# A causal convolution moved to token-major output, with one transposing transfer per block in place of a bounce through DRAM

## The chip, the cores and the metric

One core of one Trainium2 chip. The metric is the device time of one execution in microseconds; medians of several executions are quoted.

Engines in the profile: PE is TensorE (matmul), PEld its weight load, DVE VectorE, ACT ScalarE, POOL GpSimd, SP SyncE (here it only issues transfers). PEclk is the granted clock of TensorE as a share of full speed.

## The reference

```python
# x (8, 4096, 192), weight (8 heads, 7 taps), w_in (192, 2048), w_out (2048, 192), all float32
w = softmax(weight, axis=-1)                       # per head
a[b, s, h, g] = sum_k w[h, k] * x_pad[b, s + k, h, g]   # causal: 6 zero rows ahead; head = 24 channels
h = a.reshape(32768, 192) @ w_in
out = elu(h) @ w_out                               # elu: h if h > 0 else exp(h) - 1
```

## The kernel before

Tokens are handled in 32 supers of 1024 (two groups of 512). Per super there are 16 "pairs" (128 hidden units for both groups): a first matmul into PSUM, Exp on ACT, a clamp on POOL, max on DVE into `gT`. While the pairs of super s run, the second matmul of super s-1 is threaded between them, and so are two convolution steps ("conv groups" below): at pair 4 for super s+1 and at pair 12 for super s+2. The first matmul of a pair is called a hidden matmul below.

The convolution is a matmul with a band matrix made of the softmaxed taps. Before the change a window of 128 tokens of x (122 outputs and 6 tokens of history) is the stationary operand, 24 channels of one head wide, and the band is moving. Four heads run side by side in four column tiles. The result has channels on partitions.

```python
for hb in range(2):
    for (w, c0, nc_, o) in PIECES[g]:              # five windows, four of 122 columns and one of 24
        for q in range(4):                         # four heads, side by side
            h = 4 * hb + q
            ins = pe.matmul(
                H[SLOT * q : SLOT * q + CPH, k % 3, GS * hb + o : GS * hb + o + nc_],
                xg[:, s % NXB, w, CPH * h : CPH * (h + 1)],       # stationary: 128 x 24
                Tm[:, h, PAD + c0 : PAD + c0 + nc_],              # moving: 128 x 122
                start=True, stop=True, tile_position=(0, SLOT * q))
```

ACT copies this to `csb`; SP stores it to DRAM (`conv_slots`) and reads it back in the partition order that the first matmul wants (`att`): two stores and six reads a super.

The x loads are issued by POOL, which also converts float32 to bfloat16 in the transfer. A load brings four or five windows of 128 tokens, one token per partition:

```python
src = bass.AP(tensor=x_flat.tensor, offset=row * D,
              ap=[[D, P], [CW * D, w1 - w0], [1, D]])             # P = 128 rows, CW = 122
g.dma_start(xg[:, b, w0:w1, :], src).then_inc(s_x[b][part - 1], 16)
```

In the prologue the band is made by three transfers of SP: zeros to DRAM, the taps onto the diagonal, the whole read back, each with 128 rows.

## Time and profile before

Median 767.59 us (767.52 to 769.73, 3 runs); profiled span 767.1 us.

| | before |
|---|---|
| PE busy | 752.3 us, 98% |
| period of one super in the steady state | 22.65 us |
| PE time of a conv group: from the start of the matmul before it to the start of the one after it, less 0.08 us for that matmul's own 192 columns | 0.67 to 0.69 us; 64 groups in all |
| POOL busy per super | 20.45 us |
| one x load: issue on POOL, issue to landing | 0.84 us, 4.5 to 5.1 us |
| first hidden matmul (end of the prologue) | 27.4 us |

The timeline of the kernel before around one conv group, PE only (start us, us, then the group):

```profile
409.07 0.57 PE L521 MATMUL ops<-w_out,gT 64*128 64x192 f16 x10
409.58 0.65 PE L466 MATMUL H<-Tm,xg 128*24 128x122 bf16 x40
410.16 0.67 PE L521 MATMUL ops<-w_out,gT 64*128 64x192 f16 x12
```

From 409.58 to 410.16 PE belongs to the 40 conv matmuls. About 0.1 us more is lost in entering, which these starts do not show but single matmuls in the trace do.

One super of the steady state of the kernel before, in busy time (stretch: its length, then the busy time of each engine, granted clock, DMA share, GB/s):

```profile
400.00:422.65 22.65, 22.65 (x436) 15.82 (x434) 19.68 (x33) 20.12 (x36) 20.45 (x35) 1.00 0.45 98
```

PE is full. POOL comes next with 20.45 of 22.65 us: it has only 2.2 us to spare in each super.

### The profile page before, as it was taken

To read this page: it belongs to the slowest core of one execution; us is meant where nothing else is said; L and a number is where in the kernel's file an instruction comes from. 1 tells how busy PE (TensorE), PEld (TensorE's weight loads), DVE (VectorE), ACT (ScalarE), POOL (GpSimd) and SP (SyncE) were. 2 spreads that over 40 slices of the span, in tenths; PEclk is the share of its full clock that TensorE was granted. 3 is DMA by queue.
4 is the path that set the end of the run, shared out by engine and by line. 5 is a ranking of instruction groups with operands and counts; after the bars stand their busy time and mean duration, and the time that the engine had idled before them with its cause. 6 is when DMAs were issued, how large, how long until landed. Compare 5 with 4: busy or idle time off the path is not lost.

```text
span 767.1 us, 32323 instructions
## 1 busy us (share of the span) xinstructions
PE 752.3 (98%) x13910; PEld 515.0 (67%) x13910; DVE 638.7 (83%) x1035; ACT 645.2 (84%) x1155; POOL 661.8 (86%) x1109
## 2 busy tenths in 40 slices
PE   6899999999999999999999999999999999999997
PEld 3347767666766776776776677677676667767766
DVE  1588898898898898889888889888888988988993
ACT  1488888888888988888888888898888898888883
POOL 3498998899898899899889989989989988988892
PEclk8999999999999999999999999999999999999999
DMA  7474344345435435534434543543553443454211
GB/s 119 103 126 107 78 104 96 92 100 114 85 90 113 86 87 114 110 78 101 107 81 100 115 88 87 115 86 89 111 110 78 102 104 83 100 114 91 71 44 63
DMA packets 107919, 73.73 MB, mean 96 GB/s; under 512 B 45408, under 2 KB 106848, under 8 KB 107776
## 3 DMA queue, kind: packets, MB, share of 16 engines
q1 hardware_dynamic: 66344, 55.14, 23.7%
q0 software_dynamic: 40944, 16.13, 19.3%
q8 instruction: 109, 1.79, 1.0%
q10 hardware_dynamic: 488, 0.39, 0.2%
q14 instruction: 34, 0.28, 0.1%
HBM read 44.34 MB, written 42.24 MB: 113 GB/s over the span
## 4 chain that ended last, share of the span: by engine, by line
PE 93%; DMA 4%; DVE 1%; POOL 1%; ACT 0%; issue 0%; SPq 0%; POOLq 0%
PE ops L521 44%; PE H L492 44%; PE H L466 5%; DMA w_out<-in_moe_w_out_dram 1%; DMA conv_band<-wprb 1%; PE H L521 1%; DVE gT L413 1%; DMA Tk<-conv_band 1%; POOL E L310 0%; DMA wq<-in_weight_dram 0%; DMA att<-conv_slots 0%; ACT E L367 0%; DMA conv_slots<-csb 0%; POOL w_in L280 0%; PE ops L445 0%
## 5 line engine op out<-in xcount | busy, mean ns | idle before, releaser
L413 DVE SCALAR_TENSOR_TENSOR gT<-E,H 128x512 f16<-128x512 f32 x1024 | 630.6, 682 | 100.3 <-POOL E L310 92.8
L310 POOL TENSOR_SCALAR E<-E 128x512 f32<-128x512 f32 x1024 | 603.7, 612 | 71.0 <-ACT E L367 67.2
L367 ACT ACTIVATE E<-H 128x512 f32<-128x512 f32 x1024 | 546.1, 605 | 92.8 <-PE H L492 79.2
L521 PEld LDWEIGHTS ops<-w_out,gT 64*128 64x128 f16 x8064 | 342.3, 94 | 109.9 <-ACT osb L341 10.9
L521 PE MATMUL ops<-w_out,gT 64*128 64x192 f16 x8064 | 414.5, 243 | 1.1 <-DVE gT L413 0.9
L492 PE MATMUL H<-att,w_in 64*128 64x512 bf16 x3072 | 407.3, 378 | 3.5 <-DMA att<-conv_slots 2.0
L492 PEld LDWEIGHTS H<-att,w_in 64*128 64x128 bf16 x3072 | 129.8, 94 | 105.5 <-DVE gT L413 5.9
L356 ACT ACTIVATE csb<-H 128x1024 bf16<-128x1024 f32 x63 | 64.5, 1023 | 13.7 <-PE H L466 13.7
L341 ACT ACTIVATE osb<-ops 128x768 f32<-128x768 f32 x63 | 51.6, 818 | 5.1 <-PE ops L521 5.1
L275 POOL DMA_DIRECT2D xg<-in_x_dram x64 | 53.8, 842 | 0.4 <-issue 0.4
L466 PE MATMUL H<-Tm,xg 128*24 128x122 bf16 (+1 forms) x2480 | 40.7, 209 | 0.6 <-DVE gT L413 0.6
L466 PEld LDWEIGHTS H<-Tm,xg 128*24 128x24 bf16 x2480 | 31.3, 92 | 11.2 <-issue 11.2
L445 PE MATMUL ops<-zw 128*128 128x512 bf16 x86 | 24.2, 421 | 1.2 <-DVE zw L378 1.2
L445 PEld LDWEIGHTS ops<-zw 128*128 128x128 bf16 x86 | 7.8, 106 | 15.0 <-issue 8.9
L280 POOL DMA_DIRECT2D w_in<-in_moe_w_in_dram x6 | 3.5, 611 | 15.7 <-DMA att<-conv_slots 15.7
L402 DVE CAST csb<-H 128x1024 bf16<-128x1024 f32 x1 | 1.2, 1225 | 12.4 <-PE H L466 12.4
L466 PE MATMUL H<-Tk,xg 128*24 128x122 bf16 (+1 forms) x80 | 3.9, 363 | 4.7 <-DMA Tk<-conv_band 4.7
L424 DVE COPY osb<-H 128x384 f32<-128x384 f32 x1 | 0.6, 558 | 8.9 <-PE H L521 8.9
L466 PEld LDWEIGHTS H<-Tk,xg 128*24 128x24 bf16 x80 | 2.3, 117 | 6.4 <-DMA Tk<-conv_band 5.2
L521 PE MATMUL H<-w_out,gT 64*128 64x192 f16 x128 | 5.6, 243 | 0.1
L521 PEld LDWEIGHTS H<-w_out,gT 64*128 64x128 f16 x128 | 5.2, 94 | 0.3 <-PE H L521 0.3
L333 ACT ACTIVATE osb<-H 128x384 f32<-128x384 f32 x1 | 0.5, 490 | 4.7 <-PE H L521 4.7
(21 smaller groups left out, 13.3 us busy)
## 6 DMA issues: line engine op xcount, KB each, us to landing
out_dram<-osb SPq DMA_DIRECT2D x127, 192.0 KB, 2.7
conv_slots<-csb SPq DMA_DIRECT2D x64, 256.0 KB, 2.5
att<-conv_slots SPq DMA_DIRECT2D x189, 64.0 KB
xg<-in_x_dram POOLq DMA_DIRECT2D x31, 240.0 KB, 5.1
xg<-in_x_dram POOLq DMA_DIRECT2D x33, 192.0 KB, 4.5
w_in<-in_moe_w_in_dram POOLq DMA_DIRECT2D x6, 128.0 KB, 5.1
w_out<-in_moe_w_out_dram POOLq DMA_DIRECT2D x1, 768.0 KB, 9.7
w_in<-w_in POOLq DMA_DIRECT2D x1, 384.0 KB, 5.1
```

The source lines that it names most:

```text
L275: g.dma_start(xg[:, b, w0:w1, :], src).then_inc(s_x[b][part - 1], 16)
L280: g.dma_start(w_in[0:HP, j, c0:c1], bass.AP(tensor=moe_w_in.tensor, offset=8 * j * FF + c0, ap=[[CPH * FF, HEADS], [FF, 8], [1, c1 - c0]], ...
L310: g.tensor_scalar(out=E[:, n % NE, u, :], in0=E[:, n % NE, u, :], scalar1=1.0, scalar2=0.0, op0=ALU.min, op1=ALU.max,).then_inc(s_clp)
L341: a.activation(osb[:, b, :, :, :].rearrange("p g k d -> p g (k d)"), ops[:, :, 0 : 2 * D], ACT.Copy,).then_inc(s_oev)
L356: a.activation(csb[:, m % 4, :, :], H[:, slot_of_conv[m] % 3, :].rearrange("p (b t) -> p b t", b=2), ACT.Copy,).then_inc(s_ce)
L367: a.activation(E[:, n % NE, u, :], H[:, k, GS * u : GS * (u + 1)], ACT.Exp).then_inc(s_exp)
L402: v.tensor_copy(csb[:, 1, :, :], H[:, slot_of_conv[1] % 3, :].rearrange("p (b t) -> p b t", b=2),).then_inc(s_cd)
L413: v.scalar_tensor_tensor(out=gT[:, s % NG3, q, u, :], in0=E[:, n % NE, u, :], scalar=1.0, in1=H[:, slot_of_pair[n] % 3, GS * u : GS * (u + ...
L445: pe.matmul(ops[:, 0, :], zw[:, 0:P], zw[:], start=True, stop=True)
L466: ins = pe.matmul(H[SLOT * q : SLOT * q + CPH, k % 3, GS * hb + o : GS * hb + o + nc_], xg[:, s % NXB, w, CPH * h : CPH * (h + 1)], Tm[:, ...
L492: ins = pe.matmul(H[:, k % 3, GS * r : GS * (r + 1)], w_in[HP * r : HP * (r + 1), j, FC * q : FC * (q + 1)], att[HP * r : HP * (r + 1), s ...
L521: ins = pe.matmul(acc[:, g, D * kb : D * (kb + 1)], gT[HP * rt : HP * (rt + 1), t % NG3, q, g, t0 : t0 + P], w_out[HP * rt : HP * (rt + 1) ...
```

## The change

The intent: swap the operands of the convolution. The band (118 x 112) becomes stationary, and x, ten windows of one head's 24 channels (240 columns), becomes moving. Eight matmuls a super replace 80. The result has tokens on partitions; one transposing SBUF-to-SBUF transfer a super brings it to `att`, in place of two stores to DRAM and six reads. A window now has 112 outputs and 6 tokens of history, so 118 rows.

```diff
-CW = 122
+CW = 112
+KW = CW + PAD                     # 118
-NWIN = 9
+NWIN = 5                          # per group; windows of the two groups interleaved in xg
-X_AT = ((5, 1), (10, 0), (13, 2))
+X_AT = ((5, 2, 1), (13, 3, 0))
 ...
-                src = bass.AP(..., ap=[[D, P], [CW * D, w1 - w0], [1, D]])
-                g.dma_start(xg[:, b, w0:w1, :], src).then_inc(s_x[b][part - 1], 16)
+                    src = bass.AP(..., ap=[[D, rows], [CW * D, w1 - w0], [1, D]])   # rows = KW
+                    g.dma_start(
+                        xg[0:rows, b, 2 * w0 + gr : 2 * w1 : 2, :], src
+                    ).then_inc(s_x[b][gr], 16)
 ...
+                    for q in range(HU):                     # four heads
+                        h = HU * u + q
+                        ins = pe.matmul(
+                            H[0:CW, k % 3, 256 * q : 256 * q + UC],
+                            Tm[0:KW, h, :] if s else Tk[0:KW, :, h],
+                            xg[0:KW, s % NXB, :, CPH * h : CPH * (h + 1)].rearrange(
+                                "p w (j i) -> p j w i", j=3),
+                            start=True, stop=True)
 ...
+            eng.dma_start_transpose(
+                att[:, s % 2, :, :].rearrange("p j (w c) -> p (j w) c", c=CW),
+                csb[0:CW, s % 2, :],
+            ).then_inc(s_att[s % 2], 16)
 ...
-            sy.dma_start(Tk[:], band[:, :, :]).then_inc(s_band, 16)
+            sy.dma_start(Tk[0:KW, :, :], band[:, PAD : PAD + CW, :]).then_inc(s_band, 16)
```

(The other two band transfers also go from 128 to 118 rows.)

More of the change, by code (lines that the diff above doesn't have):

```diff
@@ L19 @@
 CPH = 24
-SLOT = 32
-TW = 136
-CW = 122
+CW = 112
 GS = 512
@@ L25 @@
 PAD = KSIZE - 1
-NWIN = 9
+KW = CW + PAD
+TW = CW + 2 * PAD
+NWIN = 5
+AC = NWIN * CW
+HU = 4
+UC = 2 * NWIN * CPH
 NXB = 2
@@ L31 @@
 QA = 8
-WARM = (34, 24, 2)
+WARM = (40, 24, 2)
 HALF_STEPS = (10, 10, 6, 6, 10, 11, 11)
 CONV_AT = ((4, 1, 1), (12, 2, 0))
-EARLY_CONV = {1: (1, 0), 4: (1, 1), 12: (2, 0)}
-XW = 5
-X_AT = ((5, 1), (10, 0), (13, 2))
+EARLY_CONV = {3: (1, 0), 6: (1, 1), 12: (2, 0)}
+X_AT = ((5, 2, 1), (13, 3, 0))
+ZERO_AT = 10
 W_OUT_AT = 8
-PIECES = (
-    ((0, 0, CW, 0), (1, 0, CW, CW), (2, 0, CW, 2 * CW), (3, 0, CW, 3 * CW), (4, 0, 24, 4 * CW)),
-    ((4, 24, 24, 0), (5, 0, CW, 24), (6, 0, CW, 24 + CW), (7, 0, CW, 24 + 2 * CW),
-     (8, 0, CW, 24 + 3 * CW)),
-)
 def bass_lightweight_conv__then__act_elu_kernel(
@@ L127, in bass_lightweight_conv__then__act_elu_kernel @@
                 conv_at(k, g)
-    band = nc.dram_tensor("conv_band", (P, TW, HEADS), BF16).ap()
-    bounce = nc.dram_tensor("conv_slots", (2, 2, P, SUP), BF16).ap()
+    band = nc.dram_tensor("conv_band", (KW, TW, HEADS), BF16).ap()
     with ExitStack() as stack:
@@ L141, in sema @@
             return stack.enter_context(nc.semaphore(name))
-        xg = sbuf("xg", [P, NXB, NWIN, D], BF16)
-        Tm = sbuf("Tm", [P, HEADS, TW], BF16)
-        Tk = sbuf("Tk", [P, TW, HEADS], BF16)
-        csb = sbuf("csb", [P, 4, 2, GS], BF16)
-        att = sbuf("att", [P, 2, 3, GS], BF16)
+        xg = sbuf("xg", [P, NXB, 2 * NWIN, D], BF16)
+        Tm = sbuf("Tm", [P, HEADS, CW], BF16)
+        Tk = sbuf("Tk", [P, CW, HEADS], BF16)
+        csb = sbuf("csb", [P, 2, 3 * 2 * NWIN * HP], BF16)
+        att = sbuf("att", [P, 2, 3, AC], BF16)
         w_in = sbuf("w_in", [P, 3, FF], BF16)
@@ L159, in bass_lightweight_conv__then__act_elu_kernel @@
         wprb = sbuf("wprb", [P, KSIZE, HEADS], BF16)
-        zw = sbuf("zw", [P, GS], BF16)
+        zw = sbuf("zw", [P, TW * HEADS], BF16)
         scr = sbuf("scr", [P, 2], FP32)
@@ L169, in bass_lightweight_conv__then__act_elu_kernel @@
         s_scr = sema("s_scr")
-        s_hz = sema("s_hz")
         s_x = [[sema(f"s_x{i}_{g}") for g in range(2)] for i in range(NXB)]
@@ L183, in bass_lightweight_conv__then__act_elu_kernel @@
         s_ce = sema("s_ce")
-        s_dw = [sema(f"s_dw{i}") for i in range(4)]
         s_wd = [sema(f"s_wd{i}") for i in range(2)]
-        s_tz = sema("s_tz")
         s_band = sema("s_band")
@@ L206, in bass_lightweight_conv__then__act_elu_kernel @@
         WCOLS = ((0, P * QA), (P * QA, FF))
-        NDMA_ATT = 6
-        x_need, z_need, x_count, z_count = {}, {}, [0] * NXB, 0
+        x_need, z_need, z_count = {}, {}, 0
+        x_count = [[0, 0] for _ in range(NXB)]
         for s in range(NS):
-            x_count[s % NXB] += 16 + 16 * (s == 0)
             z_count += s % SPB == 0
-            x_need[s, 0] = x_count[s % NXB]
-            x_need[s, 1] = 16 * (s // NXB + 1)
             z_need[s] = z_count
+            for g in range(2):
+                x_count[s % NXB][g] += 16 + 16 * ((s, g) in ((0, 0), (NS - 1, 1)))
+                x_need[s, g] = x_count[s % NXB][g]
         def conv_read(W, m):
@@ L229, in out_group, with conv_evac, transpose @@
             ).then_inc(s_out[b], 16)
-        def read_att(eng, W, s, g):
-            m = 2 * s + g
-            W(s_dw[m % 4], 16 * (m // 4 + 1))
-            for j in range(3):
-                src = bass.AP(
-                    tensor=bounce.tensor,
-                    offset=(2 * P * (s % 2) + 8 * j) * SUP + GS * g,
-                    ap=[[SLOT * SUP, HEADS], [SUP, 8], [1, GS]],
-                )
-                eng.dma_start(
-                    att[HP * g : HP * (g + 1), s % 2, j, :], src
-                ).then_inc(s_att[s % 2], 16)
+        def conv_evac(W, m):
+            s, u = divmod(m, 2)
+            if s >= 2:
+                W(s_att[s % 2], 16 * (s // 2))
+            return (
+                csb[0:CW, s % 2, :].rearrange("p (r h i) -> p h r i", h=HEADS, i=8)[
+                    :, HU * u : HU * (u + 1), :, :
+                ],
+                H[0:CW, slot_of_conv[m] % 3, :]
+                .rearrange("p (h c) -> p h c", h=HU)[:, :, 0:UC]
+                .rearrange("p h (r i) -> p h r i", i=8),
+            )
+        def transpose(eng, W, s):
+            for m in (2 * s, 2 * s + 1):
+                conv_read(W, m)
+            if s >= 2:
+                W(s_h, NQ * (s - 1))
+            eng.dma_start_transpose(
+                att[:, s % 2, :, :].rearrange("p j (w c) -> p (j w) c", c=CW),
+                csb[0:CW, s % 2, :],
+            ).then_inc(s_att[s % 2], 16)
         @block.gpsimd
@@ L247, in _gpsimd, with load_x @@
             W = Waits(g)
-            def load_x(s, part):
-                b, t0 = s % NXB, s * SUP
-                first = s % SPB == 0
-                if part == 0 and not first:
-                    return
-                if part == 0:
-                    if s:
-                        W(s_x[b][0], x_need[s, 0])
-                    g.memset(xg[0:PAD, b, 0, :], 0.0).then_inc(s_z)
-                    if s == 0:
-                        g.dma_start(
-                            xg[PAD:P, b, 0, :], x_flat[0 : P - PAD, :]
-                        ).then_inc(s_x[b][0], 16)
-                    return
+            def load_x(s, gr):
+                b = s % NXB
@@ L264, in load_x @@
                 if s >= NXB:
                     W(s_cv, 2 * (s - NXB) + 2)
-                if part == 1:
-                    w0, w1, row = int(s == 0), XW, t0 - PAD + CW * (s == 0)
-                else:
-                    w0, w1, row = XW, NWIN, t0 + SUP - P - CW * (NWIN - 1 - XW)
-                src = bass.AP(
-                    tensor=x_flat.tensor,
-                    offset=row * D,
-                    ap=[[D, P], [CW * D, w1 - w0], [1, D]],
-                )
-                g.dma_start(xg[:, b, w0:w1, :], src).then_inc(s_x[b][part - 1], 16)
+                first = s % SPB == 0 and gr == 0
@@ new lines, in load_x, with windows @@
+                if s == 0 and gr == 0:
+                    g.memset(xg[0:PAD, 0, 0, :], 0.0).then_inc(s_z)
+                    g.dma_start(
+                        xg[PAD:KW, 0, 0, :], x_flat[0 : KW - PAD, :]
+                    ).then_inc(s_x[0][0], 16)
+                def windows(w0, w1, rows):
+                    src = bass.AP(
+                        tensor=x_flat.tensor,
+                        offset=(s * SUP + gr * GS + w0 * CW - PAD) * D,
+                        ap=[[D, rows], [CW * D, w1 - w0], [1, D]],
+                    )
+                    g.dma_start(
+                        xg[0:rows, b, 2 * w0 + gr : 2 * w1 : 2, :], src
+                    ).then_inc(s_x[b][gr], 16)
@@ L277, in load_w_in, with batch_zeros @@
+                if s == NS - 1 and gr == 1:
+                    windows(0, NWIN - 1, KW)
+                    windows(NWIN - 1, NWIN, GS - CW * (NWIN - 1) + PAD)
+                else:
+                    windows(int(s == 0 and gr == 0), NWIN, KW)
+            def batch_zeros(s):
+                W(s_x[s % NXB][0], x_need[s, 0])
+                g.memset(xg[0:PAD, s % NXB, 0, :], 0.0).then_inc(s_z)
             def load_w_in(k):
@@ L287, in load_w_in @@
                     ).then_inc(s_w[k], 16)
-            for part in range(3):
-                load_x(0, part)
+            for gr in range(2):
+                load_x(0, gr)
             load_w_in(0)
-            for part in range(3):
-                load_x(1, part)
             W(s_w[0], 48)
@@ L296, in _gpsimd @@
             g.dma_start(w_in[HP:P, :, c0:c1], w_in[0:HP, :, c0:c1]).then_inc(s_wdp, 16)
-            W(s_att[0], 16 * NDMA_ATT)
+            W(s_cd, 1)
+            for gr in range(2):
+                load_x(1, gr)
+            W(s_att[0], 16)
             load_w_in(1)
@@ L304, in _gpsimd @@
                     ).then_inc(s_w[2], 16)
-                for at, part in X_AT:
-                    if at == i and s + NXB < NS:
-                        load_x(s + NXB, part)
+                if n == 2:
+                    load_x(2, 0)
+                for at, ahead, gr in X_AT:
+                    if at == i and s + ahead < NS:
+                        load_x(s + ahead, gr)
+                if i == ZERO_AT and (s + 2) % SPB == 0 and s + 2 < NS:
+                    batch_zeros(s + 2)
                 for u in range(2):
@@ L350, in _scalar @@
                     if m == 1:
-                        W(s_dw[0], 16)
-                        read_att(a, W, 0, 0)
                         continue
                     W(s_cv, m + 1)
-                    W(s_dw[m % 4], 16 * (m // 4))
-                    a.activation(
-                        csb[:, m % 4, :, :],
-                        H[:, slot_of_conv[m] % 3, :].rearrange("p (b t) -> p b t", b=2),
-                        ACT.Copy,
-                    ).then_inc(s_ce)
+                    a.activation(*conv_evac(W, m), ACT.Copy).then_inc(s_ce)
                 elif item[0] == "h":
@@ L378, in _vector @@
             v.memset(zw[:], 0.0).then_inc(s_zw)
-            v.memset(Tm[:], 0.0).then_inc(s_tz)
             W(s_wq, 16)
@@ L399, in _vector @@
             ).then_inc(s_set)
-            v.memset(H[:, 0:2, :], 0.0).then_inc(s_hz)
             W(s_cv, 2)
+            v.tensor_copy(*conv_evac(W, 1)).then_inc(s_cd)
             v.tensor_copy(
-                csb[:, 1, :, :],
-                H[:, slot_of_conv[1] % 3, :].rearrange("p (b t) -> p b t", b=2),
-            ).then_inc(s_cd)
-            v.tensor_copy(Tm[:, :, :].rearrange("p h t -> p t h"), Tk[:]).then_inc(s_tm)
+                Tm[0:KW, :, :].rearrange("p h t -> p t h"), Tk[0:KW, :, :]
+            ).then_inc(s_tm)
             for n in range(NP):
@@ L444, in warm @@
                 for _ in range(count):
-                    pe.matmul(ops[:, 0, :], zw[:, 0:P], zw[:], start=True, stop=True)
+                    pe.matmul(ops[:, 0, :], zw[:, 0:P], zw[:, 0:GS], start=True, stop=True)
             warm(WARM[0])
@@ L450, in _tensor @@
                     m = item[1]
-                    s, g = divmod(m, 2)
+                    s, u = divmod(m, 2)
                     if m == 0:
                         W(s_band, 48)
-                        W(s_hz, 1)
                     if m == 2:
                         W(s_tm, 1)
-                    for part in range(g + 1):
-                        W(s_x[s % NXB][part], x_need[s, part])
+                    for gr in range(2):
+                        W(s_x[s % NXB][gr], x_need[s, gr])
                     W(s_z, z_need[s])
@@ L461, in _tensor @@
                     wait_slot(k)
-                    for hb in range(2):
-                        for (w, c0, nc_, o) in PIECES[g]:
-                            for q in range(4):
-                                h = 4 * hb + q
-                                ins = pe.matmul(
-                                    H[SLOT * q : SLOT * q + CPH, k % 3,
-                                      GS * hb + o : GS * hb + o + nc_],
-                                    xg[:, s % NXB, w, CPH * h : CPH * (h + 1)],
-                                    Tm[:, h, PAD + c0 : PAD + c0 + nc_]
-                                    if s
-                                    else Tk[:, PAD + c0 : PAD + c0 + nc_, h],
-                                    start=True,
-                                    stop=True,
-                                    tile_position=(0, SLOT * q),
-                                )
+                    for q in range(HU):
[4 more added lines that the diff above has]
+                            xg[0:KW, s % NXB, :, CPH * h : CPH * (h + 1)].rearrange(
+                                "p w (j i) -> p j w i", j=3
+                            ),
+                            start=True,
+                            stop=True,
+                        )
                     ins.then_inc(s_cv)
@@ L486, in _tensor @@
                     W(s_wdp if q < QA else s_wd[1], 16)
-                    W(s_att[s % 2], 16 * NDMA_ATT * (s // 2 + 1))
+                    W(s_att[s % 2], 16 * (s // 2 + 1))
                     k = slot_of_pair[n]
@@ L494, in _tensor @@
                                 w_in[HP * r : HP * (r + 1), j, FC * q : FC * (q + 1)],
-                                att[HP * r : HP * (r + 1), s % 2, j, :],
+                                att[HP * r : HP * (r + 1), s % 2, j, 0:GS],
                                 start=(j == 0),
@@ L540, in _sync @@
             ).then_inc(s_wq, 16)
-            W(s_tz, 1)
+            W(s_zw, 1)
             sy.dma_start(
-                band[:, :, :].rearrange("p t h -> p (t h)"),
-                Tm[:, :, :].rearrange("p h t -> p (h t)"),
+                band[:, :, :].rearrange("p t h -> p (t h)"), zw[0:KW, :]
             ).then_inc(s_band, 16)
@@ L550, in _sync @@
                 offset=0,
-                ap=[[HEADS * (TW + 1), P], [1, KSIZE * HEADS]],
+                ap=[[HEADS * (TW + 1), KW], [1, KSIZE * HEADS]],
             )
-            sy.dma_start(diagonal, wprb[:].rearrange("p k h -> p (k h)")).then_inc(s_band, 16)
+            sy.dma_start(
+                diagonal, wprb[0:KW, :, :].rearrange("p k h -> p (k h)")
+            ).then_inc(s_band, 16)
             W(s_band, 32)
-            sy.dma_start(Tk[:], band[:, :, :]).then_inc(s_band, 16)
+            sy.dma_start(
+                Tk[0:KW, :, :], band[:, PAD : PAD + CW, :]
+            ).then_inc(s_band, 16)
             def copy_w(k):
@@ L564, in _sync @@
                     m = item[1]
-                    s, g = divmod(m, 2)
-                    conv_read(W, m)
-                    sy.dma_start(
-                        bounce[s % 2, :, :, GS * g : GS * (g + 1)].rearrange("b p t -> p b t"),
-                        csb[:, m % 4, :, :],
-                    ).then_inc(s_dw[m % 4], 16)
+                    s, u = divmod(m, 2)
+                    if u == 1:
+                        transpose(sy, W, s)
                     if m == 1:
-                        read_att(sy, W, 0, 1)
                         copy_w(1)
-                    elif m == 2 or g == 1:
-                        read_att(sy, W, s, g)
-                elif item[0] == "h":
-                    s, i = divmod(item[1], NQ)
-                    if i == 1 and s >= 1 and s + 1 < NS:
-                        W(s_h, NQ * s)
-                        read_att(sy, W, s + 1, 0)
                 elif item[0] == "o":
```

## The prediction

> **What bounds the kernel now.** TensorE. The page gives PE 98% busy, and 93% of the chain that ended last lies on PE: second matmul 44%, first matmul 44%, convolution 5%. In the steady state the timeline repeats every 22.65 us per super (1024 tokens). DVE (83%), ACT (84%) and POOL (86%) have room; the 16 DMA engines are about 45% busy.
>
> **What the convolution costs on PE.** In the timeline one conv group of 40 matmuls (four column tiles side by side) holds PE for about 0.68 us, from the end of streaming of the matmul before it to the start of the one after: 0.10 us to enter, ten quads 53 ns apart, 0.11 us to leave. 64 groups: about 43 us, all on the critical path.
>
> **What the change does there.** A group becomes 4 full-array matmuls of 240 columns. The 512-column warm matmuls show 2.4 columns per ns, so 240 stream in 100 ns, four in about 0.41 us. The column count hardly falls (960 for 1024): fewer instructions buy little. Entering and leaving (0.2 us) stay. Best case 0.61 for 0.68 us: 4 us over the run. Against it: a 112-column stationary. [...] The traced loads (94 ns at 128 columns, 92 at 24) don't show it. [...] I take a gain of 0 to 3 us in the steady state.
>
> **DMA.** Per super, two stores to DRAM (256 KB) and six reads (64 KB) go; one 430 KB transpose comes. It is issued after the conv at pair 4 and needed at pair 16: about 15 us of slack at 1.4 us per pair. [...] It should stay hidden. The x loads keep size and slack. ACT evacuates 960 for 1024 elements, off the critical path.
>
> **Prologue.** Before: first conv at 16.1, first hidden matmul at 27.4 us. From the conv's last matmul (20.0) the write (2.2) and reads (2.4) with gaps cost 7.4 us[...]. The first conv itself, 3.9 us in the throttled state with strided moving data, becomes about 2. Against it, the band's three transfers now have 118 partitions[...]. Net: 0 to 4 us gained.
>
> **Prediction.** 764 us, 754 to 778 holding 8 in 10. Chances: faster by over 2% 0.06, within 2% 0.82, slower by over 2% 0.12.
>
> **What would show it.** Right: PE still near 98%, super period 22.5 to 22.7 us, conv group near 0.65 us, transposes landing in 3 to 8 us, no PE wait on att after the prologue. Wrong: conv matmuls 150 ns or more apart, or weight loads well over 94 ns on PE (weights exposed); PE waiting for att (transpose over 15 us) or for xg; ACT's conv evacuation over 1.3 us.
>
> **What would make it wrong.** An exposed weight load; a far slower transpose, or one that blocks the output stores behind it; a slow prologue band.

The forecast's sum came to 764 us: 767.6 less 0 to 3 us in the steady state and 0 to 4 us in the prologue, 3.5 in the middle.

## More of the kernel before

Lines of the page of the kernel before: busy times; the granted clock in 40 slices; the queue of transfers that POOL issues (packets, MB, share of 16 engines); the chain that ended last, by engine; groups (line, engine, operation, out<-in, shapes, count | busy us, mean ns | idle just before); transfers (KB each, median us to landing).

```profile
PE 752.3 (98%) x13910; PEld 515.0 (67%) x13910; DVE 638.7 (83%) x1035; ACT 645.2 (84%) x1155; POOL 661.8 (86%) x1109
...
PEclk8999999999999999999999999999999999999999
...
q0 software_dynamic: 40944, 16.13, 19.3%
...
PE 93%; DMA 4%; DVE 1%; POOL 1%; ACT 0%; issue 0%; SPq 0%; POOLq 0%
...
L275 POOL DMA_DIRECT2D xg<-in_x_dram x64 | 53.8, 842 | 0.4 <-issue 0.4
L466 PE MATMUL H<-Tm,xg 128*24 128x122 bf16 (+1 forms) x2480 | 40.7, 209 | 0.6 <-DVE gT L413 0.6
...
xg<-in_x_dram POOLq DMA_DIRECT2D x31, 240.0 KB, 5.1
```

PE is the limit: it is busy for 98% of the span at a mean granted clock of 0.996, and 93% of the chain lies on it. The x loads appear nowhere in that chain. They cost POOL 0.84 us each and land in 5 us.

## The result and the profile after

1040.35 us median (1038.81 to 1041.85, 4 runs) for 767.9 us before. The ratio is 1.354, 95% interval 1.351 to 1.358. Ratios here are the mean time of one kernel's runs over that of the other's of the same rounds, so not quite the ratio of the medians quoted.

The same lines of the page, of the changed kernel:

```profile
PE 808.8 (78%) x11609; PEld 547.5 (53%) x11612; DVE 635.5 (61%) x1033; ACT 649.7 (62%) x1155; POOL 809.0 (78%) x1110
...
PEclk8699988899998899988889988899999889889999
...
q0 software_dynamic: 304480, 17.50, 25.9%
...
PE 58%; DMA 16%; issue 12%; POOL 6%; ACT 4%; DVE 3%
...
L271 POOL DMA_DIRECT2D xg<-in_x_dram x65 | 203.4, 3129 | 1.2 <-DVE csb L407 1.2
L467 PE MATMUL H<-xg,Tm 118*112 118x240 bf16 x248 | 47.0, 324 | 156.0 <-issue 109.5
...
xg<-in_x_dram POOLq DMA_DIRECT2D x62, 221.2 KB, 16.3
...
att<-csb SPq DMA_TRANSPOSE x32, 3.9
```

The transpose is innocent: 3.9 us to land. The x load is not. It moves fewer bytes than before (221 KB for 240), but takes 16.3 us to land for 5.1, and occupies POOL for 3.13 us for 0.84. POOL's queue carries 304,480 packets for 40,944 with about the same megabytes. PE sat idle for 156 us just before conv matmuls. Its mean granted clock fell from 0.996 to 0.913, with 32 stretches of half clock, 183 us in all.

Waits of the changed kernel (who waited for whom: total us, times, longest us):

```profile
PE H L467 <- issue: 109.5, 22, 5.9
PE H L491 <- DVE gT L417: 57.4, 32, 2.2
PE H L467 <- DMA xg<-in_x_dram: 46.5, 9, 8.3
```

The first and third lines are one wait, told apart only by whether the profile found the releaser: 22 + 9 = 31, once a super, 156 us in all, 5.0 us each. That the "issue" ones too are waits for x, the timeline shows: a load issued at 398.13 us and landing 16.1 us later frees the conv that starts at 414.27 us. The middle line is a second cost, once a super, 1.8 us.

One super of the changed kernel in four stretches (columns as before):

```profile
396.62:409.80 13.18, 11.36 (x182) 7.89 (x180) 9.86 (x17) 10.11 (x19) 12.52 (x18) 1.00 0.55 76
409.80:414.24 4.44, 0.00 (x0) 0.00 (x1) 2.15 (x4) 0.71 (x2) 4.18 (x4) 1.00 0.18 22
414.24:418.65 4.41, 4.38 (x46) 3.22 (x48) 0.39 (x1) 2.06 (x3) 1.20 (x3) 0.61 0.49 15
418.65:427.08 8.43, 8.43 (x136) 5.65 (x132) 7.26 (x13) 7.41 (x14) 7.09 (x13) 1.00 0.35 69
```

Read it downwards. In the first stretch POOL is busy 12.52 of 13.18 us and PE loses 1.8 us: POOL's 3.2 us of issue, from 398.13 us, held up the clamps. In the second PE does nothing for 4.4 us, waiting for x. In the third PE works, but at a clock of 0.61. The fourth is normal.

What the packets are: the trace lists 264,246 packets of 4 bytes on POOL's queue (1,558 before), in the steady state 4,144 to 4,148 between one load's issue and the next for 16 before, while those of 384 bytes, the rows of x, are about as many as before (39,754 for 38,906). During one load (the one issued at 398.13 us) the trace shows some 5 us in which nearly all packets are of 4 bytes, then 384-byte packets at a steady 30 to 32 per 0.5 us to the end, against up to 480 per us in the kernel before.

### The profile page after: what moved, and what is told of

Same layout as the page of the kernel before. It is cut to its first block, busy times and chain, and to the rows that moved or that the text cites. A ratio compares the mean times of both kernels' runs of the same rounds, so it can differ in the third digit from the quotient of the medians.

```text
span 1039.8 us, 27449 instructions
## 1 busy us (share of the span) xinstructions
PE 808.8 (78%) x11609; PEld 547.5 (53%) x11612; DVE 635.5 (61%) x1033; ACT 649.7 (62%) x1155; POOL 809.0 (78%) x1110
## 3 DMA queue, kind: packets, MB, share of 16 engines
q0 software_dynamic: 304480, 17.50, 25.9%
## 4 chain that ended last, share of the span: by engine, by line
PE 58%; DMA 16%; issue 12%; POOL 6%; ACT 4%; DVE 3%
PE H L491 27%; PE ops L520 27%; DMA xg<-in_x_dram 14%; PE H L467 4%; POOL E L324 3%; ACT E L374 3%; POOL xg L271 3%; DVE gT L417 3%; ACT osb L355 1%; DMA Tk<-conv_band 1%; DMA conv_band<-zw 1%; DMA conv_band<-wprb 1%; PE H L520 1%; PE ops L449 0%; DVE csb L407 0%
## 5 line engine op out<-in xcount | busy, mean ns | idle before, releaser
L491 PE MATMUL H<-att,w_in 64*128 64x512 bf16 x3072 | 428.9, 394 | 57.4 <-DVE gT L417 57.4
L520 PE MATMUL ops<-w_out,gT 64*128 64x192 f16 x8064 | 443.2, 253 | 0.9 <-DVE gT L417 0.9
L520 PEld LDWEIGHTS ops<-w_out,gT 64*128 64x128 f16 x8064 | 365.0, 99 | 128.5 <-issue 28.2
L491 PEld LDWEIGHTS H<-att,w_in 64*128 64x128 bf16 x3072 | 140.8, 98 | 162.7 <-DVE gT L417 66.2
L271 POOL DMA_DIRECT2D xg<-in_x_dram x65 | 203.4, 3129 | 1.2 <-DVE csb L407 1.2
L367 ACT ACTIVATE csb<-H 112x960 bf16<-112x960 f32 x63 | 61.2, 972 | 181.9 <-PE H L467 181.9
L467 PE MATMUL H<-xg,Tm 118*112 118x240 bf16 x248 | 47.0, 324 | 156.0 <-issue 109.5
L467 PEld LDWEIGHTS H<-xg,Tm 118*112 118x112 bf16 x248 | 29.6, 154 | 167.8 <-issue 167.8
L355 ACT ACTIVATE osb<-ops 128x768 f32<-128x768 f32 x63 | 51.3, 815 | 16.1 <-PE ops L520 15.8
L449 PE MATMUL ops<-zw 128*128 128x512 bf16 x89 | 27.6, 451 | 2.1 <-DVE zw L385 1.5
## 6 DMA issues: line engine op xcount, KB each, us to landing
xg<-in_x_dram POOLq DMA_DIRECT2D x62, 221.2 KB, 16.3
xg<-in_x_dram POOLq DMA_DIRECT2D x2, 177.0 KB, 11.3
```

Source lines behind the costliest of these rows:

```text
L271: g.dma_start(xg[0:rows, b, 2 * w0 + gr : 2 * w1 : 2, :], src).then_inc(s_x[b][gr], 16)
L355: a.activation(osb[:, b, :, :, :].rearrange("p g k d -> p g (k d)"), ops[:, :, 0 : 2 * D], ACT.Copy,).then_inc(s_oev)
L367: a.activation(*conv_evac(W, m), ACT.Copy).then_inc(s_ce)
L449: pe.matmul(ops[:, 0, :], zw[:, 0:P], zw[:, 0:GS], start=True, stop=True)
L467: ins = pe.matmul(H[0:CW, k % 3, 256 * q : 256 * q + UC], Tm[0:KW, h, :] if s else Tk[0:KW, :, h], xg[0:KW, s % NXB, :, CPH * h : CPH * (h ...
L491: ins = pe.matmul(H[:, k % 3, GS * r : GS * (r + 1)], w_in[HP * r : HP * (r + 1), j, FC * q : FC * (q + 1)], att[HP * r : HP * (r + 1), s ...
```

## The experiments

The theory (A), formed after the result: what a load of several windows costs goes by the divisors of its row count. 118 = 2 x 59 has no divisor up to 16 but 2; 128 has 16. The conjecture is that a five-window load takes 16 x 5 x rows / k packets, k the largest divisor up to 16: 4,720 for 118 rows, 640 for 128. It agrees with the two traces at hand: the 118-row load has 590 rows of x and about 4,130 packets of 4 bytes more than a load of the kernel before (4,144 to 4,148, for 16), and 590 + 4,130 is 4,720; the 128-row load has 640 rows. How the hardware comes to these counts is not shown: the packed trace does not say which engine moved a packet. So the counts and times of other row counts have to decide. (The expectations call a packet a descriptor.)

Rivals (B): the destination that skips every second window makes the load slow; or the transposes beside it do; or it is a matter of powers of two or multiples of 16.

### Only the row count of the x loads: 119, 120, 124, 128

The changed kernel with one number changed. The rows past 118 are loaded and never read.

```diff
+XR = 128                          # or 119, 120, 124
-                    windows(int(s == 0 and gr == 0), NWIN, KW)
+                    windows(int(s == 0 and gr == 0), NWIN, XR)
```

(and the same in the case of the last super)

> The changed kernel with one number changed: the x loads cover 128 partitions (ten rows nobody reads) where they covered 118. Theory A (118 has no divisor up to 16 but 2[...]): POOL's issue falls from 3.17 to about 0.85 us, landing from 16.3 to about 5.1 us, the 4-byte packets vanish but for 16 per load, PE never waits for x in the steady state, super period about 22.6 us, total about 770 us (the old 768, less 2.5 us of conv, plus 5 us of slower prologue). Theory B (the every-second-window destination, or the transposes beside it, make the loads slow): no change, above 1000 us.

> The changed kernel with x loads of 119 partitions, one more than 118. Theory A: 119 = 7 x 17, [...] 16 x 85 = 1360 for 4720; issue about 1.25 us, landing about 7 us, both inside the slack: 765 to 780 us. Theory B, or a theory by which only multiples of 16 are fast: above 1000 us.

> The changed kernel with x loads of 124 partitions. Theory A: [...] 2480 descriptors; issue about 1.9 us, landing about 10 us. The conv needs the load about 11.6 us after its issue, so little or no wait for x, but POOL's work per super becomes 18.9 + 3.8 us, as long as PE's: 770 to 810 us. Theory B: above 1000 us.

> The changed kernel with x loads of 120 partitions: 120 = 15 x 8[...], 640 descriptors, as with 128. If the largest divisor up to 16 decides, and not whether the count is a power of two or a multiple of 16: issue about 0.9 us, landing about 5.3 us, 770 to 773 us, as the run with 128 rows.

| rows | k | packets per load by theory A, 16 x 5 x rows / k | q0 packets by theory A, from the 128-row run | q0 packets measured | mean issue on POOL, us | landing, us | super period, us | time, us | ratio to before (95%) |
|---|---|---|---|---|---|---|---|---|---|
| 118 | 2 | 4,720 | 304,480 | 304,480 | 3.13 | 16.3 | 31.17 | 1040.35 | 1.354 (1.351 to 1.358) |
| 119 | 7 | 1,360 | 90,784 | 90,784 | 1.32 | 7.4 | 22.64 | 775.24 | 1.007 (1.005 to 1.008) |
| 120 | 15 | 640 | 44,992 | 44,992 | 0.94 | 5.4 | 22.57 | 771.09 | 1.002 (0.999 to 1.005) |
| 124 | 4 | 2,480 | 162,016 | 162,016 | 1.95 | 10.6 | 26.70 | 886.48 | 1.152 (1.147 to 1.157) |
| 128 | 16 | 640 | (44,992) | 44,992 | 0.91 | 5.2 | 22.57 | 771.00 | 1.001 (0.999 to 1.003) |

The packet counts are worked out so: 62 loads of five windows and 2 of four differ from the 128-row run, for 118 rows by 62 x (4,720 - 640) + 2 x (3,776 - 512) = 259,488. The counts for 118, 119, 120 and 124 rows are all met to the packet; this is a fit to five row counts, and no more is shown. (They were worked out after the runs; the packets per load for 119, 120 and 124 rows stand in the expectations.) One more row, 119 for 118, takes away 265 us. And 124, a multiple of 4 and nearer to 128, is far worse than 119. Of the orders named (row count, powers of two, multiples of 16, divisor) only the divisor fits these times. The destination, the transpose and the schedule were the same in all five.

From the pages of the runs with 119, 124 and 128 rows, in this order (of the last, the same lines as above):

```profile
q0 software_dynamic: 90784, 16.77, 22.7%
...
xg<-in_x_dram POOLq DMA_DIRECT2D x62, 223.1 KB, 7.4
```

```profile
q0 software_dynamic: 162016, 17.66, 23.9%
...
xg<-in_x_dram POOLq DMA_DIRECT2D x62, 232.5 KB, 10.6
```

```profile
PE 750.1 (98%) x11609; PEld 508.0 (66%) x11612; DVE 635.7 (83%) x1033; ACT 639.2 (83%) x1155; POOL 666.9 (87%) x1110
...
q0 software_dynamic: 44992, 17.67, 21.0%
...
L272 POOL DMA_DIRECT2D xg<-in_x_dram x65 | 59.3, 912 | 10.4 <-DVE csb L408 10.3
L468 PE MATMUL H<-xg,Tm 118*112 118x240 bf16 x248 | 38.2, 277 | 0.7 <-DVE gT L418 0.6
...
xg<-in_x_dram POOLq DMA_DIRECT2D x62, 240.0 KB, 5.2
...
att<-csb SPq DMA_TRANSPOSE x32, 5.8
```

PE is back at 98%, and its 156 us of idle time before the conv are 0.7.

The expectation for 124 rows missed: 770 to 810 us, measured 886. I had taken the slack of a load, 11.6 us, from the changed kernel, whose own stall had stretched it. In the 128-row run 9.77 us pass from POOL's issue to the start of the conv that needs the load; in the kernel before it was 9.82, so the slack could have been read there. A landing of 10.6 us (up to 14.1) overruns that, and the conv waits 2.1 us (mean of 31 waits) once a super. Slack is read from a schedule that is not already stalled.

### The old kernel with its loads cut at row 118

The kernel before, with no transpose and no skipped windows; the same bytes go to the same places.

```diff
-                g.dma_start(xg[:, b, w0:w1, :], src).then_inc(s_x[b][part - 1], 16)
+                for p0, p1 in ((0, 118), (118, P)):
+                    src = bass.AP(..., offset=(row + p0) * D,
+                                  ap=[[D, p1 - p0], [CW * D, w1 - w0], [1, D]])
+                    g.dma_start(xg[p0:p1, b, w0:w1, :], src).then_inc(s_x[b][part - 1], 16)
```

> The kernel before, untouched but for its x loads: each is cut in two, partitions 0 to 117 and 118 to 127. Same bytes to the same places, results right. Theory A: [...] issue 3.2 us (plus about 0.7 for the other part), landing about 16 us: the old kernel becomes as slow as the changed one, 1000 to 1080 us, without a transpose or a strided destination. Theory B: 768 to 790 us.

Measured: 1067.91 us, ratio 1.387 (1.385 to 1.390). From its page (the chain by line; the loads):

```profile
DMA xg<-in_x_dram 39%; PE H L493 19%; PE ops L522 18%; POOL xg L276 9%; POOL E L311 4%; PE H L467 3%; ACT E L368 2%; DVE gT L414 1%; DMA conv_slots<-csb 1%; DMA Tk<-conv_band 1%; PE H L522 1%; DMA conv_band<-wprb 0%; DMA att<-conv_slots 0%; PE ops L446 0%; DMA wq<-in_weight_dram 0%
...
xg<-in_x_dram POOLq DMA_DIRECT2D x31, 221.2 KB, 8.7
...
xg<-in_x_dram POOLq DMA_DIRECT2D x31, 18.8 KB, 14.1
```

With 118-row loads the old kernel is as slow as the new one, without the transpose and without skipped windows. The page gives the 118-row part a median landing of 8.7 us, not 16, and the small part behind it 14.1. The two share one semaphore, so the page cannot tell their landings apart; the pair lands 16.1 us after its first issue (median), near the 16 expected. No run cuts the loads at a row count with a large divisor, so that the cut itself costs little is not shown by itself.

### Two costs of the slow load, separated

The changed kernel with its 118-row loads, a third x buffer, and each load issued a whole super earlier.

```diff
-NXB = 2
+NXB = 3
-X_AT = ((5, 2, 1), (13, 3, 0))
+X_AT = ((5, 3, 1), (13, 4, 0))
```

(and earlier loads of supers 2 and 3 in the prologue)

> The changed kernel with its 118-row loads left as they were, but with a third x buffer and each load issued a whole super (22 us and more) earlier, so that its 16 us of landing is never waited for. [...] If landing time alone made the loss: about 770 us. If POOL's issue time (3.2 us, twice a super) costs too: POOL needs 18.9 + 6.3 = 25.2 us per super, more than PE's 22.6: super period 25.5 to 27 us, 860 to 900 us. No PE wait for x in either case.

(The two costs are the landing and POOL's issue time.)

Measured: 894.29 us, ratio 1.161 (1.160 to 1.163), super period 26.31 us. Two supers of it (columns as before):

```profile
400.00:426.80 26.80, 23.06 (x376) 16.54 (x374) 20.23 (x33) 20.44 (x37) 25.43 (x35) 1.00 0.52 66
426.80:453.60 26.80, 23.15 (x374) 16.44 (x372) 19.80 (x33) 20.54 (x38) 25.62 (x36) 1.00 0.65 66
```

From its page and its waits:

```profile
xg<-in_x_dram POOLq DMA_DIRECT2D x62, 221.2 KB, 16.1
...
PE H L493 <- DVE gT L419: 108.7, 58, 3.3
```

The landing is hidden now (16.1 us, and PE waits for x no more in the steady state), the granted clock is 1.00, and POOL is the limiting engine with 25.5 of 26.8 us. So the issue time by itself costs 26.31 - 22.57 = 3.74 us a super, some 116 us in all. It enters as two stalls of PE of about 1.8 us, one for each load, since DVE and then PE run out of clamped pairs.

With that the 8.6 us a super that the changed kernel loses (31.17 - 22.57) can be told apart: 5.0 us of PE waiting for x at one conv; 1.8 us of PE waiting behind POOL's issue of that same load, some 11 us earlier (398.13 us in the super above; the issue of the other load, at 411.23 us, falls inside the wait for x); and about 1.9 us of slower clock, taken as the growth of PE's busy time, (808.8 - 750.1) / 31. The sum, 8.7, is near enough.

The clock, as measured: in the changed kernel 29 of the 31 waits for x have 3.41 or 6.83 us at half clock that begin during the wait or within 0.9 us after it, 154 us together (183 us in the whole run, with the prologue and the end). After the wait of 4.4 us above, half clock ran from 415.17 us on, for 3.41 us. The stalls of 1.8 to 1.9 us in the steady state of this run were not followed by it (granted clock 1.00 in both supers above), and neither was the last wait for x of the changed kernel, 3.57 us. With the slower clock, a wait of 5.0 us in the changed kernel cost about 6.9.

### Why a load of the old kernel could give false comfort

The old kernel has one load of 122 rows (122 = 2 x 61), and it lands in 3.5 us. It has one window, so no third dimension. The prediction does not name this load. Here each load of five windows of 118 rows is issued as five of one window:

```diff
-                    src = bass.AP(..., ap=[[D, rows], [CW * D, w1 - w0], [1, D]])
-                    g.dma_start(xg[0:rows, b, 2 * w0 + gr : 2 * w1 : 2, :], src).then_inc(...)
+                    for w in range(w0, w1):
+                        row = s * SUP + gr * GS + w * CW - PAD
+                        g.dma_start(xg[0:rows, b, 2 * w + gr, :], x_flat[row : row + rows, :]).then_inc(...)
```

> The changed kernel with 118-row loads, but each load of five windows issued as five loads of one window (118 x 192, no third dimension). This asks why the old kernel's one-window load of 122 partitions misled the prediction. [...] issue about 0.55 us each (2.7 us per five), data landing within about 5 us of the last issue, no PE wait for x beyond a fraction of a us; POOL needs 18.9 + 5.5 = 24.4 us per super: super period 25 to 26 us, 845 to 875 us. [...] as slow as the changed kernel or slower, above 1030 us.

(The first figures are for the case that a one-window load is quick whatever its row count, the last for the case that 118 rows are slow in any shape. How a load is spread, no run shows.)

Measured: 860.25 us, ratio 1.118; super period 25.22 us. Its lines of the page:

```profile
q0 software_dynamic: 49056, 16.48, 19.3%
...
L268 POOL DMA_DIRECT2D xg<-in_x_dram x319 | 169.8, 543 | 14.0 <-DVE csb L404 10.4
...
xg<-in_x_dram POOLq DMA_DIRECT2D x318, 44.2 KB, 2.7
```

The same 118 rows, one window at a time, land in 2.7 us, and POOL's queue carries 49,056 packets for 304,480. Five of them share a semaphore; from the first issue to the last landing they take 6.3 us (median), where the load of five windows took 16.3. In these runs the loads of one window with 118 and 122 rows landed in 2.7 and 3.5 us, those of four or five windows with 118 rows in 11.3 and 16.3 us; why the shape matters is not shown. What is left of the loss is POOL's issue: five times 0.54 us, twice a super.

### The prologue and the weight load: a version that beats both

With 128-row x loads the changed kernel is on a par with the old one, though its super is 0.08 us shorter: its first hidden matmul starts at 30.8 us for 27.4. Start of the chain of the 128-row run (start us, us, what):

```profile
1.42 7.50 DMA conv_band<-zw
...
8.94 5.96 DMA conv_band<-wprb
...
14.92 6.87 DMA Tk<-conv_band
...
21.84 2.00 PE H L468 x8
```

Next, all three band transfers with 128 rows:

```diff
-    band = nc.dram_tensor("conv_band", (KW, TW, HEADS), BF16).ap()
+    band = nc.dram_tensor("conv_band", (P, TW, HEADS), BF16).ap()      # TW 124 -> 136
-                Tk[0:KW, :, :], band[:, PAD : PAD + CW, :]
+                Tk[:, :, :], band[:, PAD : PAD + CW, :]
```

(and P for KW in the zeroing and the diagonal)

> The 128-row x loads, and the three band transfers of the prologue with 128 rows as well (they had 118). [...] zeroing the band lands about 4 us earlier and the read back 2 us earlier, first conv near 16 us for 22, first hidden matmul near 25 to 27 us, total about 765 to 767 us, 4 us below the run with 128-row x loads alone. If those transfers are slow for another reason: 771 us again.

(The first case is that the row count makes the band's transfers slow too.)

Measured: 763.34 us, ratio 0.991 (0.989 to 0.993). The start of its chain:

```profile
0.75 3.15 DMA wq<-in_weight_dram
5.68 5.28 DMA conv_band<-wprb
10.97 3.73 DMA Tk<-conv_band
14.74 2.01 PE H L468 x8
```

The zeroing (7.50 us with 118 rows, 3.1 with 128) has left the chain; the read back fell from 6.87 to 3.73 us. The gain of 7.7 us is more than the 4 expected; the first hidden matmul now starts at 23.4 us. The traces of the changed kernel and of the kernel before show one more difference: for the zeroing with 118 rows the semaphore rises once early (1.85 us) and twice at the landing (8.80 and 8.94 us), for the kernel before's first band transfer, with 128 rows, sixteen times (4.27 to 4.94 us). What lies behind it is not shown. The zeroing has no third dimension and was slow all the same. It is SP that issues it; in these runs only one-window loads of POOL were quick in spite of their row count.

Then the stationary operand, padded with zero columns from 112 to 128:

```diff
-        Tm = sbuf("Tm", [P, HEADS, CW], BF16)
+        Tm = sbuf("Tm", [P, HEADS, P], BF16)             # zeroed once
-                            H[0:CW, k % 3, 256 * q : 256 * q + UC],
+                            H[0 : P if s else CW, k % 3, 256 * q : 256 * q + UC],
```

> As the run before it in this call, and the conv's stationary operand padded from 112 to 128 columns (zeros), into 128 output partitions. [...] the conv's weight loads fall from 130 to about 94 ns and the first two matmuls of a group stand 102 for 147 ns apart: 45 ns per group, 63 groups, 2.8 us less. If the load is not what sets that first gap: no change.

(The first case is that a load of 128 columns is as short here as the 94 ns of the matmuls' other loads.)

Measured: 761.67 us, ratio 0.989 (0.987 to 0.991). The weight loads of the 128-row run with the wide band:

```profile
L468 PEld LDWEIGHTS H<-xg,Tm 118*112 118x112 bf16 x248 | 23.7, 129 | 11.4 <-issue 10.8
```

and of this one:

```profile
L471 PEld LDWEIGHTS H<-xg,Tm 118*128 118x128 bf16 x248 | 19.2, 97 | 12.3 <-issue 11.1
```

The load of 128 columns took 97 ns, that of 112 columns 129. A conv group falls from 643 to 611 ns, the super from 22.57 to 22.51 us (median; 22.53 on average). The drop of 1.7 us of the total is about what 62 groups at 32 ns give (2.0), but the runs of the two kernels overlap (761.95 to 764.68 and 759.66 to 762.92), and the two profiles differ in the prologue as well: the mean granted clock was 0.997 in the earlier one and 0.999 in this one, a warm-up matmul took 429 and 419 ns in the mean, and this one's first hidden matmul starts at 22.4 us for 23.4. So the group is the evidence and not the total.

Last, fewer warm-up matmuls (matmuls on zeros whose result nobody reads) before the first hidden matmul:

```diff
-WARM = (40, 24, 2)
+WARM = (40, 15, 2)
```

> As the 128-column run, with 15 for 24 warm-up matmuls between the first conv and the first hidden matmul. In the run with 128-row x loads these 24 were on the chain (6.4 us) while the transpose had landed about 1.9 us before their end. Expected: 1.5 to 2 us less than the 128-column run, if the clock is granted in full as early as before; more if not. Some 760 to 763 us, below the old kernel's 770.

Measured: 761.68 us: no gain. In both profiles the transpose lands at 22.3 us and the first hidden matmul starts at 22.4. With 24 warm-up matmuls, 419 ns each in the mean over that profile, they end just before; with 15, 434 ns each in the mean, PE waits 0.7 us for the transpose. The expectation was taken from a run in which they took 439 ns each in the mean and ended after the transpose had landed.

## Why the prediction was wrong

It forecast 764 us, within 2%; the kernel took 1040.

- **The step that failed** is "The x loads keep size and slack." The size kept, near enough; the duration did not. 118 rows in a load with a window dimension made 4,720 packets for 640: landing 16.3 us for 5.1, issue on POOL 3.13 us for 0.84. The slack stayed at 9.8 us; it and POOL's 2.2 us of spare time were both overrun. The prediction feared 118 rows in the band's three transfers of the prologue, but did not ask the same of the 64 loads in the loop. Undoing it alone (128 rows) brings 771.0 us.
- **The transpose: right.** It landed in 3.8 us at best, 3.9 (changed kernel) or 5.8 us (128-row run) in the median; the range given was 3 to 8. PE did not wait for `att` after the prologue.
- **The conv on PE: right.** 0.643 us a group where PE did not wait, for "near 0.65"; the weight load of 112 columns takes 129 ns and is hidden but for the first of a group (147 ns to the second matmul, 102 after that). That load is "well over 94 ns", which the prediction listed as a sign of being wrong; it cost 45 ns a group.
- **Super period 22.5 to 22.7 us**: right once the x loads are mended (22.57); 31.17 in the kernel as changed.
- **The prologue: the cost was seen, the balance missed.** The gain of 0 to 4 us became a loss of 5 (32.5 us for 27.4) with 118 rows, and a gain of 4 (23.4 us) with 128.
- **What would make it wrong** listed the transpose, the weight load and the band. PE waiting for xg was named as a sign, but with no cause behind it; the 12% for "slower by over 2%" was not tied to it.

## What to carry to other kernels

When a change alters a partition count, factor the new count for every transfer that carries it: in these runs the packets and the time of POOL's loads of several windows went with the largest divisor up to 16 (landing 16.3 us at 118 rows, 10.6 at 124, 7.4 at 119, 5.4 at 120, 5.2 at 128), SP's zeroing of the band took 7.50 us with 118 rows and 3.1 with 128, and only POOL's loads of one window escaped (2.7 us with 118). Padding the x loads to 120 or 128 rows cost nothing next to that (771 us for 1040). Fewer bytes did not mean less time (221 KB in 16.3 us, 240 KB in 5.2). Charge a transfer that POOL issues twice, for landing and for issue time, which grew here with the packets (0.91 us for 640, 3.13 us for 4,720). And read slack from a schedule that does not already stall.
